# Two-level products of a fused attention and Fourier-mix kernel: later sums made among the products, conversion not emptied at a chunk's end, three loaded blocks in the last unit

## The chip, the cores and the metric

The kernel runs on one core of a Trainium2 chip. A core has TensorE (matmuls; its weight loads are listed apart as PEld), VectorE (DVE), ScalarE (ACT), GpSimd (POOL) and SyncE (SP, which here only issues DMAs). The metric is device time in microseconds. The kernel before took 2447.19 us (median of three runs, 2444.5 to 2452.97).

## The reference, cut to what matters

An attention block (batch 8, 12 heads, 448 rows, head size 64, heads mixed before and after the softmax) makes `x`; a Fourier mix, a normalisation and a two-layer network follow. The change lies in the last lines alone.

```python
X = np.fft.fft(np.fft.fft(x, axis=1), axis=2)
u = x + np.real(X).astype(np.float32)
un = (u - mu) / np.sqrt(var + 1e-06)
ch = np.maximum(un @ w_ch1, 0.0) @ w_ch2      # 768 x 3072 and 3072 x 768, given as float64
return (u + ch).astype(np.float32)
```

## The kernel before, in words

**Tiles and stages.** First comes the attention with the Fourier mix (`mix_phase`). Then `ffn_phase` works through the network in six chunks of its 3072 inner columns (`NC = 6`); in each chunk it passes over the 3584 rows in seven blocks of 512 (`NTB = 7`). A chunk and a block make a unit `n`, with `c, t = divmod(n, NTB)`, 42 in all. A unit has two halves. `first` multiplies the block by the chunk's part of `w_ch1`, applies the ReLU and leaves the result in `h`; `second` or `second2` multiplies `h` by the chunk's part of `w_ch2` and adds the result to the output in DRAM.

**Products by sevens.** Both multiplications split each matrix in 2 x 2 and make seven products of sums of blocks in place of eight. The sums of the weights are made while they are converted from float64 (`_Weights`); those of the inner result are `hs1`, `hs2`, `h21` and `h12s` (lines 1066 to 1068 and 1078). From chunk 2 on (`DEEP = 2`), the second multiplication is split once more: each of the seven products is made as seven again of half the size (`second2`). For this the four sums of each of the seven inner blocks are needed, `hq` (`quarter`, line 990), and of the weights `wt` (`halves`, line 999, in the first unit of a chunk, in turn on VectorE and GpSimd).

**The order.** From chunk 2 on the program writes out the order of TensorE, VectorE, ScalarE and GpSimd by hand; each engine takes its instructions in that order. `second2` gives each piece of work a step `s`. Product `j` of `ORDER2` begins at step `7 j` and makes its seven matmuls at `7 j` + 0, 3, 4, 5, 8, 13 and 16, so that three products overlap; at the same steps ScalarE copies sums out of PSUM (`take`, line 1185), VectorE adds to them (`more`, line 1179), and whole results are added (`both`, line 1188). The matmul at `7 j + 16` adds to the PSUM sum `P` that `more(j, 3, "P")` of step `7 j + 11` reads, and so must wait for it. Steps from 49 on are made during the next unit's first half, at the places that `SEAM` gives (the seam). An output block goes out as a DMA that adds to DRAM, from GpSimd's queue (`out_`, line 1191).

**Sums of the inner result, before.** After product 6 of the first half GpSimd makes the four sums of H11 and H22 together (128 x 256 each). After product 2 VectorE makes `hs1`, `hs2` and `h21` and at once the four sums of H21, HS1 and HS2 together (128 x 384 each). After the last product VectorE makes `h12s`, and GpSimd the four sums of H12 and H12S. All of VectorE's share stands in front of the adds of `second2`.

**Conversion.** A part of a weight matrix (25 parts for chunks 1 to 5) is converted on VectorE in 32 instructions (lines 235 to 267): four pieces of seven, and four sums. `wts.add` queues a part, `wts.deal(n)` issues the next `n` instructions, and with them loads, and stores left from the call before. Those DMAs go through GpSimd's queue up to chunk 1, later through SP's. Chunk 1 deals 18 in the first half and 28 in the second and queues ten parts in its seven units; two-level units but the first of a chunk deal 18 (`DEALS`, after products 0 to 4). After the first half of a two-level chunk's last unit, `wts.deal(1000)` issues whatever is queued. In that unit too the next chunk's weights are loaded, in the buffers that its products leave (`load_w1`, `load_w2`).

**The last unit.** (`end`.) Two output blocks are loaded and added to in SBUF: (0, 0) in the tile of product 1 and (0, 1) in that of product 2, the last of all. They are stored at the end without adding DMAs; (1, 0) and (1, 1) go out as adding DMAs. GpSimd makes two of the whole-tile adds, at steps 34 and 47, both into the tile of the last product.

## Time and profile before

| what | value |
|---|---|
| median of three runs | 2447.19 us (2444.5 to 2452.97) |
| the profiled execution's own time | 2442.24 us |
| its span, from first to last instruction | 2440.46 us |
| mean granted TensorE clock | 0.981 |
| busy: PE, PEld, DVE, ACT, POOL | 2324.3, 1749.7, 1707.8, 1130.4, 1099.9 us |
| TensorE's first matmul of the network | 861.2 us from the span's start |
| first unit of chunk 1, of chunk 2 | 1151.33 us, 1408.55 us |

Engines are named PE, PEld, DVE, ACT, POOL and SP; `L1179` is line 1179 of the kernel before. A line of the timeline gives start, duration, engine, line, operation, output and inputs, shapes and count, and in brackets the idle time ahead with what ended it. A stretch in the table by stage is given in microseconds from the span's start. Durations of successive instructions can overlap a little, so the distance from start to start is used where several are added up.

### The profile page before, as it was taken

How to read it: one execution, taken by the hardware profiler on the slowest of the kernel's cores; microseconds unless marked ns; L12 is line 12 of the kernel's file. 1: busy time of each engine (PE TensorE's matmuls, PEld its weight loads, DVE VectorE, ACT ScalarE, POOL GpSimd, SP SyncE). 2: the span in 40 equal slices, each digit the busy share in tenths (PEclk: the TensorE clock that was granted, in tenths of full speed). 3: DMA queues.
4: the chain of work that ended last, by engine and by line, in shares of the span. 5: the costliest groups of instructions: out<-in, count | busy, mean ns of one | idle time of the engine just before them, and what ended most of it. 6: DMA issues, size and time to landing. Idle time of an engine off the chain costs nothing.

```text
span 2440.5 us, 59595 instructions
## 1 busy us (share of the span) xinstructions
PE 2324.3 (95%) x22856; PEld 1749.7 (72%) x22856; DVE 1707.8 (70%) x3414; ACT 1130.4 (46%) x3097; POOL 1099.9 (45%) x1557
## 2 busy tenths in 40 slices
PE   6999999999999699999999999998999899999998
PEld 3555555555555477677777689987899789998997
DVE  4888888888897557775676667676767677555445
ACT  4776777666677332231222234433344244344443
POOL 3697787977777241210334242233323333333323
PEclk8999999999999899999999999998999899999999
DMA  7555564655554645658687865575655946674553
GB/s 168 167 177 171 179 189 158 186 171 171 175 165 155 214 152 193 212 177 308 184 231 193 273 186 136 163 212 172 182 135 144 261 111 167 159 201 103 143 117 65
DMA packets 216616, 428.65 MB, mean 176 GB/s; under 512 B 39054, under 2 KB 138406, under 8 KB 216334
## 3 DMA queue, kind: packets, MB, share of 16 engines
q1 hardware_dynamic: 146574, 286.38, 34.1%
q0 software_dynamic: 63904, 136.70, 25.6%
q8 instruction: 183, 3.00, 0.5%
q10 hardware_dynamic: 5856, 1.77, 0.4%
q14 instruction: 99, 0.81, 0.1%
HBM read 212.76 MB, written 129.39 MB: 140 GB/s over the span
## 4 chain that ended last, share of the span: by engine, by line
PE 78%; DVE 11%; DMA 5%; ACT 2%; POOL 2%; issue 1%; SPq 1%; ACTq 0%; DVEq 0%; POOLq 0%
PE psP L1026 14%; PE psP L1159 8%; PE psR L1026 7%; PE mx L486 6%; PE psP L1102 6%; PE ms L547 5%; PE ms L459 5%; PE po L520 5%; PE psR L1159 4%; PE psQ L1026 4%; DMA Kr<-Sb 3%; PE psR L1102 3%; DVE hq L990 2%; PE psQ L1159 2%; PE ms L661 2%; PE psQ L1102 1%
## 5 line engine op out<-in xcount | busy, mean ns | idle before, releaser
L1026 PE MATMUL psP<-ub,w1t 128*128 128x256 f32 x2016 | 481.6, 380 | 0.0
L1026 PEld LDWEIGHTS psP<-ub,w1t 128*128 128x128 f32 x2016 | 380.3, 191 | 48.6 <-issue 0.6
L510 POOL TENSOR_SCALAR PP<-PP,rcp 128x448 f32<-128x448 f32 x384 | 254.5, 672 | 219.5 <-DVE rcp L508 188.1
L500 ACT ACTIVATE PP<-mx,nmx 128x448 f32<-128x448 f32 x384 | 240.7, 632 | 162.9 <-DVE nmx L493 151.3
L1191 POOL DMA_DIRECT2D out_dram<-od x110 | 134.5, 1416 | 361.9 <-DVE od L1179 163.5
L493 DVE TENSOR_REDUCE nmx<-mx 128x1 f32<-128x448 f32 x384 | 223.0, 617 | 86.7 <-PE mx L486 84.9
L486 PE MATMUL mx<-Kr,kw 60*32 60x448 f32 x3072 | 231.8, 550 | 16.7 <-DMA Kr<-Sb 12.8
L1026 PE MATMUL psR<-ub,w1t 128*128 128x256 f32 x1008 | 231.3, 379 | 0.0
L1188 DVE TENSOR_TENSOR od<-od 128x768 f32<-128x768 f32 x194 | 186.6, 973 | 55.2 <-ACT od L1185 54.2
L990 POOL TENSOR_TENSOR hq<-h 128x256 f32<-128x256 f32 x112 | 83.6, 746 | 305.2 <-issue 169.2
L531 DVE STREAM_TRANSPOSE Pv<-po 128x896 f32<-128x896 f32 x192 | 212.7, 1108 | 9.4 <-PE po L520 6.5
L520 PE MATMUL po<-PP,kw 60*32 60x448 f32 x3072 | 213.3, 539 | 2.9 <-POOL PP L510 2.0
L1185 ACT COPY od<-psP 128x192 f32<-128x192 f32 x388 | 124.3, 320 | 186.1 <-PE psP L1159 185.2
L1026 PEld LDWEIGHTS psR<-ub,w1t 128*128 128x128 f32 x1008 | 191.4, 190 | 25.9
L459 PE MATMUL ms<-kT,qT 64*32 64x448 f32 (+1 forms) x3072 | 202.6, 544 | 7.2 <-ACT qT L330 6.3
L330 ACT COPY Sb<-ms 124x448 f32<-124x448 f32 x384 | 184.0, 542 | 36.1 <-DMA Kr<-Sb 21.4
L547 PEld LDWEIGHTS ms<-Pv,vv 64*64 64x64 f32 x5376 | 143.5, 133 | 69.9 <-issue 33.8
L213 POOL DMA_DIRECT2D raw<-in_moe_w_ch_dram x80 | 48.8, 612 | 262.9 <-DVE tmp L257 252.0
L547 PE MATMUL ms<-Pv,vv 64*64 64x120 f32 x5376 | 166.3, 269 | 0.3 <-issue 0.2
L1102 PE MATMUL psP<-w2t,h 128*128 128x384 f32 x448 | 155.2, 490 | 2.2 <-DVE od L1122 2.2
L1159 PE MATMUL psP<-wt,h 128*128 128x192 f32 x392 | 101.5, 341 | 43.4 <-DVE od L1179 43.4
L1045 DVE TENSOR_TENSOR h<-h,psP 128x512 f32<-128x512 f32 x42 | 28.9, 688 | 161.6 <-PE psP L1026 161.3
(140 smaller groups left out, 4516.9 us busy)
## 6 DMA issues: line engine op xcount, KB each, us to landing
ub<-ub SPq DMA_DIRECT2D x294, 384.0 KB
Kr<-Sb SPq DMA_DIRECT2D x768, 105.0 KB
out_dram<-od POOLq DMA_DIRECT2D x138, 384.0 KB, 6.6
w1t<-w SPq DMA_DIRECT2D x42, 384.0 KB
w2t<-w SPq DMA_DIRECT2D x42, 384.0 KB
raw<-in_moe_w_ch_dram POOLq DMA_DIRECT2D x48, 256.0 KB, 5.3
raw<-in_moe_w_ch_dram POOLq DMA_DIRECT2D x32, 384.0 KB, 7.3
w<-wst POOLq DMA_DIRECT2D x84, 128.0 KB, 3.6
```

Source lines behind the costliest of these rows:

```text
L459: nc.tensor.matmul(pss[x][o:o + hi - lo, :S], st["qT", xx][64 * x:64 * x + 64, y, lo:hi], st["kT", xx][64 * x:64 * x + 64, y, :], start=Tr ...
L486: nc.tensor.matmul(mx[x][64 * z + o:64 * z + o + 32, :S], kw1[64 * x:64 * x + KR, o:o + 32], Kr[64 * x:64 * x + KR, z, :], start=True, sto ...
L493: nc.vector.tensor_reduce(nmx[:, :], steps[T]["mx"][x][:, :S], axis=AX.X, op=ALU.max, negate=True)
L500: nc.scalar.activation(steps[T]["PP"][:, x, :], steps[T]["mx"][x][:, :S], ACTF.Exp, bias=steps[T]["nmx", x][:, :], accum_out=steps[T]["den ...
L510: nc.gpsimd.tensor_scalar(PP[:, x, :], PP[:, x, :], rcp[:, x:x + 1], 1.0, op0=ALU.mult, op1=ALU.mult)
L520: nc.tensor.matmul(po[o:o + 32, z, :S], kw2[64 * z:64 * z + KR, y, :], PP[64 * z:64 * z + KR, :, c * HS:(c + 1) * HS], start=True, stop=True)
L531: nc.vector.transpose(g["Pv"][:, T % GT, :].rearrange("p (z s) -> p z s", z=2), steps[T]["po"][:, :, :S])
L547: nc.tensor.matmul(pss[y][64 * x:64 * x + 64, :nu * R], st["v", pr][64 * y:64 * y + 64, x, jb * D:(jb + 1) * D], _ap(Pv, 64 * y * rp + 32 ...
L1026: nc.tensor.matmul(p[:, m, :], w1[i][:, kc, m * P:(m + 1) * P], ub[:, kc, :], start=i in (0, 4, 1)[:3 - seed] and m == kc == 0, stop=kc == ...
L1102: nc.tensor.matmul(p, h[:, LHS[i], kf, x * P:(x + 1) * P], w2[i][:, kf, :], start=i in (0, 4, 1)[:3 - (c > 0)] and kf == 0, stop=kf == FM ...
L1159: nc.tensor.matmul(ps[j, key][:, :DQ], a, b, start=m in (0, 4), stop=True, skip_group_check=True)
L1188: eng.tensor_tensor(D[j][:, :, :], D[j][:, :, :], D[k][:, :, :], op=ALU.add)
```

## The change

- **Conversion.** `wts.deal(1000)` at the end of the two-level chunks is gone, and that at the end of chunk 1. Chunk 1 deals 24 in the first half (4 for 3) beside 28 in the second, and queues parts until there are 52 instructions: twelve parts in place of ten. Two-level units deal 14 in place of 18, and the first of a chunk 8 in place of none. A last `deal(0)` issues stores that are left.
- **Sums.** `quarters` makes the four sums of one or more blocks at once. In front of the second half VectorE makes only those of HS2 (128 x 128 each), between `hs2` and `h21`. Those of H21 come at step 12 of `second2` and those of HS1 at step 19, both on VectorE; `h12s` at step 20. GpSimd makes those of H12 right after the last product of the first half, without waiting for `h12s`, and those of H12S after step 20.
- **Last unit.** Three blocks are loaded in tiles of their own: (0, 0), (0, 1) and (1, 1). The last product adds into the tile of (0, 1); product 1 is copied out by ScalarE and added as a whole. VectorE makes seven whole-tile adds in place of five, GpSimd two (steps 34 and 41, into two tiles), and (1, 1) is stored, at step 48, where it went out as an adding DMA. The pool of output tiles has nine buffers in place of seven.

```diff
-DEALS = (2, 4, 4, 4, 4, 0, 0)
+DEALS = ((0, 2, 2, 2, 2, 0, 0), (2, 3, 3, 3, 3, 0, 0))
...
-    def quarter(eng, hq, h, f0, f1, s):
+    def quarters(eng, hq, h, f0, f1):
...
-                    for x in range(4):
-                        quarter(nc.gpsimd, hq, h, H11, H22 + 1, x)
+                    quarters(nc.gpsimd, hq, h, H11, H22 + 1)
...
-            if deep and t:
-                wts.deal(DEALS[k])
-            elif i != 2 and not deep:
-                wts.deal(2 if norms else 3)
+            if deep:
+                wts.deal(DEALS[t > 0][k])
+            elif i != 2:
+                wts.deal(2 if norms else 3 if c == 0 else 4)
             if i == 2:
                 vec.tensor_tensor(hs1, h21, h22, op=ALU.add)
                 vec.tensor_tensor(hs2, hs1, h11, op=ALU.subtract)
+                if deep:
+                    quarters(vec, hq, h, HS2, HS2 + 1)
                 vec.tensor_tensor(h21, h11, h21, op=ALU.subtract)
-                if deep:
-                    for x in range(4):
-                        quarter(vec, hq, h, H21, HS2 + 1, x)
...
-        vec.tensor_tensor(h12s, h12, hs2, op=ALU.subtract)
         if deep:
-            for x in range(4):
-                quarter(nc.gpsimd, hq, h, H12, H12S + 1, x)
-        if t == NTB - 1 and deep:
-            wts.deal(1000)
+            quarters(nc.gpsimd, hq, h, H12, H12 + 1)
+            wts.deal(0)
+        else:
+            vec.tensor_tensor(h12s, h12, hs2, op=ALU.subtract)
...
         def part(j, q):
+            if end and j == 6:
+                j = 8
...
-            if end and j in (5, 6):
+            if end and j == 6:
                 more(j, q, key)
...
+        v11, v12, v22 = range(7, 10)
+        on(12, lambda: quarters(vec, st["hq"], st["h"], H21, H21 + 1))
+        on(19, lambda: quarters(vec, st["hq"], st["h"], HS1, HS1 + 1))
+        on(20, lambda: vec.tensor_tensor(st["h"][:, H12S], st["h"][:, H12],
+                                         st["h"][:, HS2], op=ALU.subtract))
+        on(20, lambda: quarters(pl, st["hq"], st["h"], H12S, H12S + 1))
         if end:
-            on(0, load, j1, 0, 0)
-            on(0, load, j2, 0, 1)
-            for s, *o in ((19, vec, j1, j0), (33, vec, j5, j0), (34, pl, j2, j5),
-                          (40, vec, j6, j5), (41, vec, j3, j6), (47, vec, j6, j4),
-                          (47, pl, j2, j4)):
+            for v, r, d in ((v11, 0, 0), (v12, 0, 1), (v22, 1, 1)):
+                on(0, load, v, r, d)
+            for s, *o in ((24, vec, v11, j0), (33, vec, j5, j0), (34, pl, v12, j5),
+                          (40, vec, j6, j5), (41, vec, j3, j6), (41, pl, v22, j6),
+                          (47, vec, v22, j4), (48, vec, v12, j4), (54, vec, v11, j1)):
                 on(s, both, *o)
             on(42, out_, j3, 1, 0)
-            on(48, out_, j6, 1, 1)
-            on(7 * j1 + 19, store, j1, 0, 0)
-            on(7 * j2 + 19, store, j2, 0, 1)
+            on(48, store, v22, 1, 1)
+            on(55, store, v11, 0, 0)
+            on(61, store, v12, 0, 1)
...
-            for _ in range(0 if c == 0 else 2 if t < 3 else 1):
+            while c and sum(o[1] for o in wts.ops) < 52:
                 wts.add(*parts_.pop(0))
...
-            if c == 0 or t == NTB - 1:
+            if c == 0:
                 wts.deal(1000)
...
-                for name, bufs in (("wt", 1), ("hq", 1), ("od", 7)):
+                for name, bufs in (("wt", 1), ("hq", 1), ("od", 9)):
...
-            while parts_ and sum(o[1] for o in wts.ops) < sum(DEALS):
+            while parts_ and sum(o[1] for o in wts.ops) < 14:
                 wts.add(*parts_.pop(0))
```

More of the change, by code (lines that the diff above doesn't have):

```diff
@@ L985, in quarter @@
                               for x in range(2) for f in range(2))
-        to, a, b, op = ((o[:, :, 0], a21, a22, ALU.add),
-                        (o[:, :, 1], o[:, :, 0], a11, ALU.subtract),
-                        (o[:, :, 2], a11, a21, ALU.subtract),
-                        (o[:, :, 3], a12, o[:, :, 1], ALU.subtract))[s]
-        eng.tensor_tensor(to, a, b, op=op)
+        for to, a, b, op in ((o[:, :, 0], a21, a22, ALU.add),
+                             (o[:, :, 1], o[:, :, 0], a11, ALU.subtract),
+                             (o[:, :, 2], a11, a21, ALU.subtract),
+                             (o[:, :, 3], a12, o[:, :, 1], ALU.subtract)):
+            eng.tensor_tensor(to, a, b, op=op)
     def halves(i, eng):
```

## The prediction

> **What bounds the kernel now.** I read the page first, then who waited for whom on TensorE from the first two-level unit to the end, then a table by stage whose stretches are units. A unit is 512 rows of one chunk; its length is from its first matmul of line 1026 to the next unit's.
>
> ```profile
> span 2440.5 us, 59595 instructions
> ```
>
> ```profile
> PE psP L1159 <- DVE od L1179: 44.2, 30, 12.5
> ```
>
> The change touches only what follows the attention: one-level chunk 1 and two-level chunks 2 to 5. In the latter TensorE loses 44.2 us in 30 waits, all for line 1179: the VectorE add that reads a PSUM sum before matmul 3 of the same product may add to it. So VectorE's lateness at one place is the loss, not its load.
>
> The stages; columns are stretch and length, busy time of PE, PEld, DVE, ACT, POOL, granted clock, DMA share, GB/s:
>
> ```profile
> 1151.33:1368.47 217.14, 217.14 (x841) 159.60 (x840) 141.87 (x335) 53.36 (x101) 78.77 (x114) 1.00 0.77 209
> 1368.47:1408.55 40.08, 37.89 (x142) 27.08 (x141) 27.60 (x66) 8.96 (x17) 9.39 (x13) 0.97 0.90 302
> 1408.55:1444.59 36.04, 33.50 (x175) 30.79 (x174) 17.88 (x34) 14.64 (x41) 19.23 (x27) 0.99 0.58 167
> 1444.59:1618.58 173.99, 172.36 (x912) 159.16 (x911) 121.17 (x246) 74.97 (x211) 53.13 (x60) 1.00 0.59 157
> 1618.58:1669.89 51.31, 37.26 (x184) 34.41 (x183) 35.47 (x70) 14.97 (x43) 11.16 (x12) 0.87 0.80 250
> 1669.89:1708.51 38.62, 36.05 (x184) 33.41 (x183) 25.19 (x48) 15.00 (x43) 21.11 (x24) 0.96 0.56 137
> 1708.51:1883.12 174.61, 172.36 (x912) 159.15 (x911) 124.29 (x246) 74.98 (x211) 53.52 (x60) 1.00 0.59 156
> 1883.12:1932.52 49.40, 37.45 (x184) 34.60 (x183) 32.21 (x70) 14.98 (x43) 10.77 (x12) 0.86 0.82 254
> 1932.52:1971.24 38.72, 36.15 (x185) 33.51 (x184) 25.20 (x48) 15.00 (x43) 21.09 (x24) 0.96 0.56 135
> 1971.24:2180.46 209.22, 206.83 (x1093) 190.97 (x1093) 135.50 (x251) 89.87 (x253) 64.12 (x72) 1.00 0.61 166
> 2180.46:2219.19 38.73, 36.16 (x185) 33.51 (x184) 25.18 (x48) 15.00 (x43) 21.09 (x24) 0.96 0.55 136
> 2219.19:2392.61 173.42, 172.36 (x911) 159.15 (x911) 87.86 (x156) 74.95 (x211) 52.62 (x60) 1.00 0.48 117
> 2392.61:2440.46 47.85, 36.48 (x192) 32.92 (x190) 22.43 (x45) 13.28 (x37) 17.24 (x16) 0.92 0.44 83
> ```
>
> Five quiet units of chunk 5 take 173.42 us with PE busy 172.36: 34.47 us is a unit without a gap (172.36 / 5). Against that, chunk 2's last unit is 16.84 too long and chunk 3's 14.93; the first units of chunks 3, 4 and 5 are 4.15, 4.25 and 4.26 too long, and chunk 2's has 2.54 idle; the other 21 units before the last, in four rows, are 1.63 + 2.25 + 2.40 + 1.06 = 7.3 too long. The gaps behind this, on TensorE's timeline (a drain, another, a chunk's first unit, an ordinary unit; the fifth row is matmul 3 of the third product of that ordinary unit):
>
> ```profile
> 1656.45 1.01 PE L1159 MATMUL psP<-wt,h 128*128 128x192 f32 x2 [12.54 <-DVE od L1179]
> ```
> ```profile
> 1918.89 1.01 PE L1159 MATMUL psP<-wt,h 128*128 128x192 f32 x2 [10.53 <-DVE od L1179]
> ```
> ```profile
> 2206.68 0.59 PE L1159 MATMUL psP<-wt,h 128*128 128x192 f32 x2 [2.57 <-DVE od L1179]
> ```
> ```profile
> 2416.47 0.59 PE L1159 MATMUL psP<-wt,h 128*128 128x192 f32 x2 [0.21 <-DVE od L1179]
> ...
> 2421.12 0.49 PE L1159 MATMUL psP<-wt,h 128*128 128x192 f32 x2
> ```
>
> A gap of 2.57 makes a unit 4.26 longer, for the clock falls after it. Two pairs of neighbouring stretches:
>
> ```profile
> 1429.68:1433.10 3.42, 1.54 (x10) 1.25 (x8) 3.35 (x9) 1.22 (x4) 0.61 (x1) 1.00 0.02 7
> 1433.10:1436.51 3.41, 2.75 (x17) 2.75 (x18) 1.66 (x6) 1.58 (x5) 2.83 (x4) 1.00 0.00 0
> 2204.51:2207.92 3.41, 1.24 (x7) 1.24 (x8) 2.61 (x9) 0.61 (x2) 1.40 (x2) 1.00 0.01 2
> 2207.93:2211.33 3.40, 3.40 (x12) 3.40 (x12) 0.71 (x2) 1.27 (x5) 1.41 (x3) 0.50 0.01 2
> ```
>
> 1.88 us idle in such a stretch (3.42 - 1.54) left the clock at 1.00; 2.17 (3.41 - 1.24) was followed by one at 0.50. [...]
>
> **The parts of the change, one by one.** *The drain.* Lines 1082 and 1083, which empty the conversion at a chunk's end, go. At the end of chunks 2 and 3 they put 20 conversion instructions (18 dealt in each of six units out of four steps of 32) between the first half's sums and the add of line 1179: the gaps of 12.54 and 10.53, smaller ones ahead, and the half clock behind. All of 16.84 + 14.93 = 31.8 us goes if the work finds cover. It moves to three places. (a) Chunk 1 deals 52 a unit for 46: 6 more at 0.42 (141.87 / 335) are 2.5 us, beside 12.5 us in which VectorE idles per unit ((217.14 - 141.87) / 6). TensorE has no gap there, so this costs nothing; without that cover it would be 2.5 x 7 = 18. GpSimd issues these loads and stores, in order behind the accumulating writes, as now. (b) Ordinary two-level units deal 14 for 18, which only helps. (c) First units of chunks deal 8, now none:
>
> ```profile
> 2195.01 0.69 DVE L1045 TENSOR_TENSOR h<-h,psP 128x512 f32<-128x512 f32 x1 [3.28 <-PE psP L1026]
> 2197.50 0.69 DVE L1051 TENSOR_TENSOR h<-h,psR 128x512 f32<-128x512 f32 x1 [1.80 <-PE psR L1026]
> ...
> 2201.92 0.83 DVE L990 TENSOR_TENSOR hq<-h 128x384 f32<-128x384 f32 x1
> ...
> 2204.48 0.35 DVE L999 TENSOR_TENSOR wt<-w2t 128x192 f32<-128x192 f32 x1
> ...
> 2205.67 0.69 DVE L1078 TENSOR_TENSOR h<-h 128x512 f32<-128x512 f32 x1
> 2206.28 0.35 DVE L1179 TENSOR_TENSOR od<-od,psP 128x192 f32<-128x192 f32 x1
> ```
>
> Six fall into the 3.28 us idle before line 1045 and two into the 1.80 after it: at 0.42, 2.5 and 0.8. At the 0.6 of the drain (12.54 / 20) 3.6 would overrun the first by 0.3, which the second takes up. Their loads and stores stand on SP behind the weight loads of the seam and before the next `ub` loads; SP would wait only if VectorE fell behind, and the DMA share is 0.56 there against 0.80 in the unit they leave. The last dealt step, in chunk 4's last unit, stores chunk 5's weights during the fifth product of seven, a whole half before they are loaded.
>
> *The sums in ordinary units.* The front is what VectorE does between the last ReLU it waits for and the first add of line 1179:
>
> ```profile
> 2413.45 0.56 DVE L990 TENSOR_TENSOR hq<-h 128x384 f32<-128x384 f32 x1
> ...
> 2415.46 0.69 DVE L1078 TENSOR_TENSOR h<-h 128x512 f32<-128x512 f32 x1
> 2416.06 0.35 DVE L1179 TENSOR_TENSOR od<-od,psP 128x192 f32<-128x192 f32 x1
> ```
> ```profile
> L999 DVE TENSOR_TENSOR wt<-w2t,wt x32: 350/357/746, 1398.8 to 2205.4; 128x192 f32<-128x192 f32 x32
> ```
> ```profile
> L990 POOL TENSOR_TENSOR hq<-h x112: 712/726/1441, 1423.5 to 2417.7; 128x256 f32<-128x256 f32 x112
> ```
>
> Four sums of 384 take 2.01 us (2413.45 to 2415.46), `h12s` 0.60. In their place stand four of 128. No row has that size: 192 takes 0.35 and 384 0.56, so a straight line gives 0.28; bounds 0.2 and, with GpSimd in the way, 0.75 (the 746 of the row). I take 0.30, near the smallest row. The front shortens by 2.61 - 1.20 = 1.4 against a gap of 0.21 (up to 0.7 elsewhere), so it closes with 1.2 to spare. GpSimd's four sums of H12 now come earlier, beside these, and at 0.4 each (three overlaps) would eat that 1.2 and no more. Next in line is the sum of the second and third product: eight sums, `h12s` and three adds of 0.35 now stand between the first add and the third product's, 2.4 + 0.7 + 1.1 = 4.2 us, where TensorE needs 4.65 (2416.47 to 2421.12): they fit. GpSimd's four more, smaller instructions add at most 4 x 0.73 us per unit, of which it is busy for 10.5 (52.62 / 5) in 34.5. Of the 7.3 us I take 7.0; bounds 3 and 7.3.
>
> [...]
>
> *The sums in first units of a chunk.* There the front also holds four weight differences, and GpSimd works throughout, so four sums took 2.56 us (2201.92 to 2204.48). Four of 128 at the same 1.5-fold price (0.83 / 0.56) take 1.8; `h12s` (0.61) goes too: 1.4 less. GpSimd's H12 sums, now before and not after it, can lengthen the weight differences by 0 to 4 x 0.4; I take 0.2, for the row's median lies at its minimum. The gap falls from 2.57 to 1.4, below the 1.88 that left the clock whole. The four units together are 15.2 too long (4.15 + 4.25 + 4.26 + 2.54); 4 x 1.4 = 5.6 stay, 9.6 go. Bounds 0 and 12.4 (0.7 left in each).
>
> *Chunk 1's last unit.* 40.08 for 36.19 (217.14 / 6): VectorE stood for the new chunk's weights.
>
> ```profile
> 1398.30 0.36 DVE L999 TENSOR_TENSOR wt<-w2t 128x192 f32<-128x192 f32 x1 [4.80 <-DMA w2t<-w]
> ```
>
> Nothing in the change frees that load, and as many dealt instructions stand behind it (28 in the half for 26, though narrower). I take 0; bounds 3.9 gained and 4 lost, a second gap of that size with its clock.
>
> *The last unit.* Now the last product adds into a tile that GpSimd is adding to:
>
> ```profile
> 2428.55 2.26 POOL L1188 TENSOR_TENSOR od<-od 128x768 f32<-128x768 f32 x1
> ```
> ```profile
> 2430.84 0.35 DVE L1179 TENSOR_TENSOR od<-od,psQ 128x192 f32<-128x192 f32 x1 [1.78 <-POOL od L1188]
> ```
> ```profile
> 2432.04 0.59 PE L1159 MATMUL psP<-wt,h 128*128 128x192 f32 x2 [2.55 <-DVE od L1179]
> ```
> ```profile
> L1188 DVE TENSOR_TENSOR od<-od 128x768 f32<-128x768 f32 x194 | 186.6, 973 | 55.2 <-ACT od L1185 54.2
> ```
>
> After the change its last GpSimd add is one product earlier and into another tile. VectorE gets two whole-tile adds more (2 x 0.97) and gives four adds of 0.35 to ScalarE: 0.5 more. 2.55 - 0.5 is about 2.0; with its front's 0.2, 2.2. Bounds 0 and 3. The third loaded block is read during the first half and hidden there; two more buffers cost no time.
>
> *Sum.* 31.8 + 7.0 + 9.6 + 0 + 2.2 = 50.6 us. The profiled execution took 2442.24 (span 2440.46 and 1.8 around it), so 2391.6 like for like. The runs shown were 2444.5 to 2452.97, median 2447.19, 4.95 above the profiled one; with the same distance 2396.6, so I say 2396.
>
> **The rivals.** *Chunk starts stay.* GpSimd's earlier sums shut VectorE out, whole instructions at a time, where both are busiest: four times 0.4, plus a dealt store late. The gap stays above 2 us with its half clock, the 9.6 do not come, and chunk 1's end loses 2 more: 39 saved, 2408. For it: the 0.83 and 746 rows. Against: the median of 357. 20%.
>
> *More than I count.* Narrower conversions (256 wide, for 384) behind the weight wait close chunk 1's last gap (3.9), and chunk starts keep 0.7 only (2.8): 57.3 saved, 2390. 13%.
>
> *Slower: the sums among the products hold TensorE in all 28 units.* At s per 128-wide sum the third product's add comes 12 s - 5.3 us late: 8 s + 0.69 + 1.05 against 4.65, and at the front 4 s against 2.61 less its gap of 0.21. From s = 0.54 this costs over 1.2 per unit and so more than the 34 us that the drains and the last unit give; at 0.60 it is 1.9, the clock halves (4.26 - 2.57 = 1.7 more), and 28 x 3.6 - 34 is 67 more, 2514. For it: fixed costs could make 128 as dear as 384 (0.56). Against: 192 takes 0.35. 3%.
>
> *The work only moves.* The 20 instructions come up again in front of an add of line 1179, and the kernel stays at 2447. It would have to be in first units, whose idle 3.28 and 1.80 speak against it. 2%.
>
> **How the numbers follow.** My case has 62%, with 2389 to 2404 of its own: 4 us for chunk starts, 4 for chunk 1's end, 3 for ordinary units, not all one way. 20%, 13%, 3% and 2% for the others. The range takes in 2390 and 2408 and, as the runs spread by -2.7 and +5.8 about their median, ends at 2386 and 2412. About 0.3% (7 us) is what a measurement can tell from no change; faster holds the first three cases: 0.95, same 0.02, slower 0.03.
>
> **What would show it.** Right: the last units of chunks 2 and 3 at 34.5 to 35 with clock 1.00; ordinary units at 34.5; chunk starts at 35.5 to 36.5 without a half clock; chunk 1's last unit near 40; the last gap under 1 us; 128-wide sums on VectorE at 0.3. Wrong: waits for line 1179 at the second or third product, half-clock stretches at chunk starts, a wait for conversion stores in first units, or chunk 1's units over 36.2.

## The result and the profile after

| | before | after |
|---|---|---|
| median, us | 2446.59 (4 runs, 2444.5 to 2452.97) | 2385.86 (4 runs, 2384.69 to 2390.02) |
| the profiled execution, us | 2442.24 | 2384.91 |
| its mean granted clock | 0.981 | 0.991 |

The ratio is 0.9751, with a 95% interval of 0.9729 to 0.9772. The forecast was 2396 (2386 to 2412): the direction and the main mechanism held, and the time came out 0.14 us under the range.

Line 1178 of the kernel after is line 1179 of before (VectorE's add), 1156 is 1159 (the seven matmuls), 1187 is 1188, 1119 is 1122. The page of the kernel after:

```profile
span 2383.1 us, 59994 instructions
```

Who waited for whom on TensorE from chunk 1 to the end (us in total, times, longest):

```profile
PE psP L1156 <- DVE od L1178: 11.1, 6, 2.7
PE psP L1026 <- DVE h L1045: 0.2, 1, 0.2
```

Of 44.2 us in 30 waits, 11.1 in 6 are left. The stages, cut at the same places as before (stretch and length, busy time of PE, PEld, DVE, ACT, POOL, clock, DMA share, GB/s):

```profile
1152.94:1370.57 217.63, 217.41 (x842) 159.52 (x840) 156.51 (x371) 53.38 (x101) 86.04 (x125) 1.00 0.82 221
1370.57:1406.78 36.21, 36.21 (x141) 26.52 (x140) 24.98 (x64) 8.96 (x17) 12.12 (x21) 1.00 0.95 319
1406.78:1441.75 34.97, 33.18 (x176) 30.53 (x175) 25.27 (x60) 14.64 (x41) 19.92 (x29) 1.00 0.66 196
1441.75:1612.77 171.02, 171.02 (x912) 159.28 (x911) 121.70 (x266) 74.98 (x211) 59.67 (x80) 1.00 0.60 158
1612.77:1646.97 34.20, 34.20 (x183) 31.85 (x183) 25.68 (x54) 14.99 (x43) 11.99 (x16) 1.00 0.93 285
1646.97:1684.12 37.15, 34.48 (x185) 31.84 (x183) 32.21 (x64) 15.01 (x43) 22.20 (x28) 1.00 0.65 173
1684.12:1855.14 171.02, 171.02 (x912) 159.29 (x911) 121.22 (x266) 74.98 (x211) 59.89 (x80) 1.00 0.59 155
1855.14:1889.34 34.20, 34.20 (x183) 31.85 (x183) 23.71 (x54) 14.99 (x43) 12.03 (x16) 1.00 0.92 286
1889.34:1925.88 36.54, 34.48 (x185) 31.84 (x183) 30.89 (x64) 15.00 (x43) 22.26 (x28) 1.00 0.65 165
1925.88:2131.11 205.23, 205.23 (x1094) 191.15 (x1094) 150.16 (x319) 89.98 (x253) 73.72 (x96) 1.00 0.64 176
2131.11:2167.39 36.28, 34.47 (x183) 31.82 (x183) 26.32 (x56) 14.99 (x43) 21.22 (x28) 1.00 0.62 158
2167.39:2338.41 171.02, 171.02 (x912) 159.28 (x911) 93.81 (x196) 74.97 (x211) 59.24 (x80) 1.00 0.51 123
2338.41:2383.13 44.72, 36.18 (x192) 32.97 (x190) 25.02 (x51) 14.55 (x41) 17.99 (x19) 0.95 0.41 80
```

Where length and PE's busy time agree, TensorE never waited. They agree in all ordinary two-level units and in both last units that used to drain, at 34.20 us a unit. Length less busy time is the gap: 1.79, 2.67, 2.06 and 1.81 us at the starts of chunks 2 to 5. The two tables, row against row:

| part | before to after, us | saved | forecast |
|---|---|---|---|
| last units of chunks 2 and 3 | 100.71 to 68.40 | 32.3 | 31.8 |
| 21 ordinary units | 731.24 to 718.29 | 12.9 | 7.0 |
| first units of chunks 2 to 5 | 152.11 to 144.94 | 7.2 | 9.6 |
| chunk 1's last unit | 40.08 to 36.21 | 3.9 | 0 |
| the last unit, to the span's end | 47.85 to 44.72 | 3.1 | 2.2 |
| chunk 1's six other units | 217.14 to 217.63 | -0.5 | 0 |
| all ahead of chunk 1 | 1151.33 to 1152.94 | -1.6 | 0 |
| sum | 2440.46 to 2383.13 | 57.3 | 50.6 |

The last line but one is not the change's doing. The part ahead of chunk 1 is the same in all kernels of this study, and its end lies anywhere from 1150.0 to 1160.0 us in their profiles. A spread of that size is in every comparison of whole runs, so the sections below also use the time from chunk 1's first matmul to the end: 1289.1 us before, 1230.2 after.

VectorE's sums of line 990 (ns: least, median, most):

```profile
L990 DVE TENSOR_TENSOR hq<-h x168: 275/284/676, 1425.9 to 2363.1; 128x128 f32<-128x128 f32 x168
```

A 128-wide sum takes 0.28 (forecast 0.30), but up to 0.676. Where, VectorE's timeline at the start of chunk 3 shows:

```profile
1667.83 0.56 DVE L990 TENSOR_TENSOR hq<-h 128x128 f32<-128x128 f32 x1
1668.43 0.63 DVE L990 TENSOR_TENSOR hq<-hq,h 128x128 f32<-128x128 f32 x1
1668.99 0.68 DVE L990 TENSOR_TENSOR hq<-h 128x128 f32<-128x128 f32 x1
1669.58 0.68 DVE L990 TENSOR_TENSOR hq<-h,hq 128x128 f32<-128x128 f32 x1
...
1671.05 0.60 DVE L999 TENSOR_TENSOR wt<-w2t 128x192 f32<-128x192 f32 x1
...
1672.63 0.35 DVE L999 TENSOR_TENSOR wt<-w2t,wt 128x192 f32<-128x192 f32 x1
1672.90 0.34 DVE L1178 TENSOR_TENSOR od<-od,psP 128x192 f32<-128x192 f32 x1
1673.16 0.28 DVE L990 TENSOR_TENSOR hq<-h 128x128 f32<-128x128 f32 x1
```

Four sums take 2.35 us (1667.83 to 1670.18, where the next instruction begins) for a forecast of 1.8, four weight differences 1.85 for 1.4 at 0.35 each. The first sum after them is at 0.28 again. At chunks 4 and 5 the four sums take 2.15 and 2.14 us, the four differences 1.85 and 1.86.

### The profile page after: what moved, and what is told of

The parts are those of the page before. It is cut to its first block, busy times and chain, and to the rows that moved or that the text cites. A ratio compares the mean times of both kernels' runs of the same rounds, so it can differ in the third digit from the quotient of the medians.

```text
span 2383.1 us, 59994 instructions
## 1 busy us (share of the span) xinstructions
PE 2307.2 (97%) x22856; PEld 1740.8 (73%) x22856; DVE 1739.4 (73%) x3636; ACT 1131.5 (47%) x3101; POOL 1145.6 (48%) x1684
## 4 chain that ended last, share of the span: by engine, by line
PE 85%; DMA 4%; DVE 4%; POOL 2%; issue 2%; ACT 1%; SPq 1%; ACTq 0%; POOLq 0%; DVEq 0%
PE psP L1026 17%; PE psP L1156 10%; PE psR L1026 9%; PE mx L486 7%; PE ms L547 6%; PE psP L1099 6%; PE ms L459 5%; PE po L520 5%; PE psR L1156 5%; PE psQ L1026 4%; PE psR L1099 3%; DMA Kr<-Sb 3%; PE psQ L1156 2%; PE ms L661 2%; PE psQ L1099 1%
## 5 line engine op out<-in xcount | busy, mean ns | idle before, releaser
L990 POOL TENSOR_TENSOR hq<-h 128x256 f32<-128x256 f32 (+1 forms) x168 | 104.3, 621 | 293.4 <-ACT h L1046 173.2
L1187 DVE TENSOR_TENSOR od<-od 128x768 f32<-128x768 f32 x196 | 188.6, 974 | 52.4 <-ACT od L1184 50.6
L459 PEld LDWEIGHTS ms<-kT,qT 64*32 64x32 f32 (+1 forms) x3072 | 67.9, 106 | 79.9 <-issue 51.8
```

The lines of the kernel that those rows point to most:

```text
L459: nc.tensor.matmul(pss[x][o:o + hi - lo, :S], st["qT", xx][64 * x:64 * x + 64, y, lo:hi], st["kT", xx][64 * x:64 * x + 64, y, :], start=Tr ...
L1187: eng.tensor_tensor(D[j][:, :, :], D[j][:, :, :], D[k][:, :, :], op=ALU.add)
```

## The experiments

The theory was that the moved sums closed the ordinary units' gaps, that 0.27 us of the forecast 34.47 belongs to the wait itself, and that the chunk starts are long because VectorE and GpSimd shut each other out (the sums of 0.56 to 0.68 us for 0.28 above). Its rivals lay the shorter units to the thinner dealing or to the two more output buffers, and the chunk starts to VectorE's own work there. What moved chunk 1's end was open. (In the expectations, "the planner" is what sets the order of instructions where chunk 1's work and chunk 2's meet; by what rule it does so stays open.) First the three edits alone, then the price of a gap, then chunk starts and chunk 1's end.

**The sums alone.** The kernel before, with the sums of the inner result moved and nothing else:

```diff
+                    quarters(vec, hq, h, HS2, HS2 + 1)
...
-            for x in range(4):
-                quarter(nc.gpsimd, hq, h, H12, H12S + 1, x)
+            quarters(nc.gpsimd, hq, h, H12, H12 + 1)
...
+        on(12, lambda: quarters(vec, st["hq"], st["h"], H21, H21 + 1))
+        on(19, lambda: quarters(vec, st["hq"], st["h"], HS1, HS1 + 1))
...
```

> Only the sums are moved; conversion, chunk ends and last unit as before. Theory A (a wait of TensorE costs its listed gap and some 0.27 us more, in which its pipeline of matmuls empties and fills): ordinary two-level units 34.20, as after the whole change, though only 0.21 to 0.7 of gap is removed from units of 34.7 to 35.2; together about 13 us. Theory B (the 0.27 below my gapless 34.47 comes from the fewer dealt instructions, the nine output buffers or other traffic): ordinary units at 34.47. Both: the last units of chunks 2 and 3 keep gaps of 11 and 9, chunk 1's last unit stays at 40.1, chunk starts fall to 36 to 37.5. Span 2417 by A, 2423 by B.

Measured: 2417.76 (before beside it 2443.66), ratio 0.9894, 0.9871 to 0.9918. Two of its stages: chunk 2's last unit, and the five ordinary units of chunk 5.

```profile
1620.85:1669.13 48.28, 36.69 (x184) 33.84 (x183) 35.79 (x78) 14.98 (x43) 11.76 (x16) 0.89 0.85 265
2200.44:2371.46 171.02, 171.02 (x912) 159.28 (x911) 93.90 (x196) 74.97 (x211) 59.30 (x80) 1.00 0.50 118
```

The drains stay, at 48.28 and 45.96, and the ordinary units are at 34.20: it is the sums that bring these down. The chunk starts take 34.96 and three times 36.29, without a half clock. Chunk 1's last unit takes 38.57, not the expected 40.1: its gap of 2.01 halved no clock.

**The conversion alone.**

```diff
-DEALS = (2, 4, 4, 4, 4, 0, 0)
+DEALS = ((0, 2, 2, 2, 2, 0, 0), (2, 3, 3, 3, 3, 0, 0))
...
-        if t == NTB - 1 and deep:
-            wts.deal(1000)
+        if deep:
+            wts.deal(0)
...
-            for _ in range(0 if c == 0 else 2 if t < 3 else 1):
+            while c and sum(o[1] for o in wts.ops) < 52:
...
```

> Only the conversion is changed; sums and last unit as before. Both theories: the last units of chunks 2 and 3 fall from 51.3 and 49.4 to 34.7. Theory A: ordinary units stay at 34.68, with the gap of 0.21; theory B: 34.4. On chunk 1's last unit: if its gap went because chunk 1 now converts other, narrower parts there, it falls from 40.1 to 36.2 in this kernel too; if the sums did it through the order that the planner chose at that seam, it stays at 40.1. Chunk starts at 38 to 39.5, with eight dealt instructions more and the old sums. Span about 2403.

Measured: 2411.39 beside 2443.66, ratio 0.9876, 0.9854 to 0.9899. Chunk 1's last unit, chunk 2's last, chunk 3's first, and the five ordinary ones:

```profile
1367.46:1403.84 36.38, 36.38 (x142) 26.52 (x141) 24.99 (x64) 8.96 (x17) 12.13 (x21) 1.00 0.94 316
1614.81:1649.62 34.81, 34.47 (x183) 31.83 (x183) 24.37 (x46) 14.99 (x43) 10.66 (x12) 1.00 0.93 289
1649.62:1690.38 40.76, 37.43 (x184) 34.79 (x183) 30.67 (x56) 15.00 (x43) 22.28 (x24) 0.92 0.58 150
2183.42:2356.86 173.44, 172.37 (x913) 159.16 (x912) 87.78 (x156) 74.97 (x211) 52.61 (x60) 1.00 0.49 117
```

The drains are gone, and chunk 1's end with them. The eight dealt instructions of a first unit aren't free: the gap at chunk 3's start rises from 2.57 (38.62 - 36.05) to 3.33. Of the four starts, 37.40, 40.76, 38.77 and 37.05, only the third lies in the expected 38 to 39.5. And the bare price of a wait stands in these rows: 34.47 busy in 34.81 us, 0.27 over the 34.20 of a unit without a gap, beside a gap of 0.34.

**The last unit alone.**

```diff
-            on(48, out_, j6, 1, 1)
+            on(48, store, v22, 1, 1)
...
-                for name, bufs in (("wt", 1), ("hq", 1), ("od", 7)):
+                for name, bufs in (("wt", 1), ("hq", 1), ("od", 9)):
```

(with the other lines of the last unit in the change.)

> Only the last unit and the nine output buffers. The last unit shortens by 2.6 (after the whole change it was 3.1 shorter, 0.5 of it the gap in its front), all else stays: ordinary units 34.68. Were the buffers behind the 0.27 (theory B), ordinary units would be at 34.4 and the span 6 us shorter still. Span 2437.8 by A, 2431 by B.

Measured: 2440.31 beside 2443.66, ratio 0.999, 0.9975 to 1.0004: not told from no change by the runs. By its profile the last unit went from 47.85 to 45.28, the 2.6 less that were expected; the five ordinary units:

```profile
2220.28:2393.71 173.43, 172.36 (x912) 159.15 (x911) 87.85 (x156) 74.96 (x211) 52.65 (x60) 1.00 0.50 121
```

They are as before, so the two buffers more aren't what shortened them.

From chunk 1's first matmul the three alone gain 29.2, 35.6 and 1.7 us, 66.5 together; 6.5 of the sums' 29.2 come out of the drains (51.31 to 48.28, 49.40 to 45.96), which the conversion edit takes anyway. The 60.0 left is near the 58.9 of the whole change.

**What a gap costs.** The kernel after, with one of VectorE's sums ahead of the first add repeated 6 to 26 times in the ordinary units of chunks 4 and 5 (a repeat writes the same result again):

```diff
+LADDER = {29: 6, 30: 10, 31: 14, 32: 18, 33: 22, 34: 26, 36: 8, 37: 12, 38: 16, 39: 20, 40: 24}
...
+                for _ in range(LADDER.get(n, 0)):
+                    vec.tensor_tensor(hq[:, HS2, 3], h[:, HS2, 1, :P], hq[:, HS2, 1],
+                                      op=ALU.subtract)
```

> The changed kernel, in which VectorE repeats one sum of 128 (the last of HS2, with the same result) a number of times in the front of the 11 ordinary units of chunks 4 and 5: 6, 10, 14, 18, 22, 26 and 8, 12, 16, 20, 24 times. The first 6 or 7 should cost nothing (the spare time that I worked out is 1.2 to 1.5 us), each further one 0.2. Theory A: a unit takes 34.20 + gap + 0.27 for any gap, so a step of 0.27 at the first gap and slope 1. Theory B: 34.20 + gap. Half clock: where over about 2 us idle fall into one stretch of 3.41 us, 1.6 more; where the gap straddles two stretches, none, as in the chunk start whose gap of 2.67 left the clock whole.

Measured: one run, 2456.98. A repeat cost 0.33, not the 0.2 assumed, so that six of them already made a gap, and no unit between zero and six repeats was seen. Units with 6 repeats, 10, none (a chunk's start), and 8:

```profile
1922.69:1958.51 35.82, 34.48 (x185) 31.84 (x184) 25.53 (x60) 15.00 (x43) 12.05 (x16) 1.00 0.55 147
1958.51:1997.51 39.00, 36.15 (x184) 33.51 (x184) 28.21 (x64) 15.00 (x43) 12.00 (x16) 0.96 0.57 154
2168.76:2205.07 36.31, 34.48 (x185) 31.84 (x183) 26.34 (x56) 15.00 (x43) 21.23 (x28) 1.00 0.60 146
2205.07:2243.13 38.06, 36.15 (x184) 33.51 (x184) 21.34 (x48) 15.00 (x43) 11.88 (x16) 0.96 0.47 114
```

The gaps are 1.34, 2.85, 1.83 and 1.91 us. A gap of 1.34 or 1.83 costs itself and 0.27 or 0.28; one of 1.91 itself and 1.95. So a gap has two extra prices: 0.27 in each of these units, and, where about 1.9 us of idle time fall into one stretch of 3.41, the half clock. The stretches around the 1.83 and the 1.91:

```profile
2191.05:2194.45 3.40, 1.57 (x10) 1.27 (x9) 3.33 (x9) 1.03 (x4) 2.31 (x4) 1.00 0.25 86
2194.46:2197.87 3.41, 3.41 (x22) 3.41 (x22) 3.21 (x12) 2.29 (x8) 0.53 (x2) 1.00 0.00 0
2228.56:2231.97 3.41, 1.50 (x9) 1.35 (x9) 3.21 (x14) 0.93 (x4) 0.00 (x0) 1.00 0.00 0
2231.98:2235.38 3.40, 3.40 (x13) 3.40 (x12) 2.16 (x8) 1.18 (x4) 1.66 (x4) 0.50 0.00 0
```

1.83 us idle in a stretch of 3.40 left the clock whole (the next is at 1.00), 1.91 in one of 3.41 halved it for the next.

**Weight differences later.** The last of the seven parts of `halves` in a chunk's first unit goes behind the second product's add:

```diff
-            if deep and t == 0:
+            if deep and t == 0 and k < 6:
...
+        if t == 0:
+            on(26, halves, ORDER2[6], vec)
```

> The changed kernel; in the first unit of a chunk the four weight differences of the last product, which VectorE makes in the front, are made at step 26 of the second half. Theory A (the gaps of 1.8 to 2.7 that are left at chunk starts are the lateness of VectorE's front): the front is 1.85 to 2.2 us shorter and the gaps fall to 0 to 0.8; units of 34.2 to 35.3 for 36.3 to 37.2. Theory B (something else is late next: the differences now stand before the adds of the fourth and fifth product, or the GpSimd sums are): a wait of 1 us or more appears at a later product, and the units stay over 36.

Measured: one run, 2381.84; 1223.0 us from chunk 1's first matmul. The starts of chunks 2 to 5 are 33.11, 34.53, 34.67 and 34.43 (34.97, 37.15, 36.54 and 36.28 after). With the four weight differences out of the front the gaps are as good as gone; chunk 1's last unit got a gap of 0.89 instead.

**GpSimd's H12 sums later.** In first units alone, behind step 20, where `h12s`'s sums stand:

```diff
-            quarters(nc.gpsimd, hq, h, H12, H12 + 1)
+            if t:
+                quarters(nc.gpsimd, hq, h, H12, H12 + 1)
...
+        if t == 0:
+            on(20, lambda: quarters(pl, st["hq"], st["h"], H12, H12S + 1))
...
```

> The changed kernel; in the first unit of a chunk GpSimd makes the sums of H12 only with those of H12S, behind h12s, as before the change. Theory A (GpSimd's sums shut VectorE out for whole instructions): the four weight differences in the front take 1.2 us for 1.85, the gaps at chunk starts fall by 0.6 to 0.7, while the four sums of HS2 stay at 0.56 to 0.68 each, for GpSimd's own weight differences run beside them. Theory B (the differences are slow for another reason): no change. The later sums of H12 (3.6 us for eight) could make product H12 wait, which would show as a wait of TensorE for GpSimd.

Measured: one run, 2383.22. The gaps fall to 0.88, 1.66, 1.14 and 0.89, by 0.9 to 1.0 each. VectorE's timeline at the place of the one shown of after:

```profile
1671.46 0.74 DVE L999 TENSOR_TENSOR wt<-w2t 128x192 f32<-128x192 f32 x1
1672.24 0.36 DVE L999 TENSOR_TENSOR wt<-w2t,wt 128x192 f32<-128x192 f32 x1
...
1672.78 0.35 DVE L999 TENSOR_TENSOR wt<-w2t,wt 128x192 f32<-128x192 f32 x1
1673.05 0.35 DVE L1179 TENSOR_TENSOR od<-od,psP 128x192 f32<-128x192 f32 x1
```

The weight differences but the first are back at 0.35, and the four take 1.59 us to the add (line 1179 here) for 1.85. At chunk 4 the two add up to the gap's fall of 0.92: the differences take 1.19 for 1.85, and the four sums 1.89 for 2.15. VectorE's instructions are the same in number and size; only GpSimd's sums went from beside them.

**Chunk 1's conversion as before.** Two-level units keep their gain, chunk 1 deals and queues as before:

```diff
-                wts.deal(2 if norms else 3 if c == 0 else 4)
+                wts.deal(2 if norms else 3)
...
-            while c and sum(o[1] for o in wts.ops) < 52:
+            for _ in range(0 if c == 0 else 2 if t < 3 else 1):
```

(with the rest dealt in later units, 17 for 14.)

> The changed kernel, but chunk 1 deals and queues as before (46 a unit, ten parts, so that its last unit converts 384 wide), and two-level units deal 17 for 14 to make up. Theory A (chunk 1's last gap went because narrower instructions and fewer weight differences now stand ahead of the adds there): it comes back, 39 to 40 us for 36.2. Theory B (the sums or the planner's order elsewhere closed it): it stays at 36.2. Ordinary units 34.2 to 34.5, since 17 dealt leave VectorE less spare time.

Measured: one run, 2398.2; 1237.0 us from chunk 1's first matmul. Chunk 1's last unit is 37.17 with a gap of 0.72, between the two theories' 39 to 40 and 36.2: four weight differences, not eight, stand ahead of the add here too (table below). A few ordinary units with 17 dealt instructions rise to 34.9 to 36.3.

**Weight differences earlier and later.** Four of the seven parts one product earlier or more, the last one as in the experiment above:

```diff
-                halves(ORDER2[k], (nc.vector, nc.gpsimd)[k % 2])
+                for x in ((0,), (1,), (2,), (3,), (4, 5), (), ())[k]:
+                    halves(ORDER2[x], (nc.vector, nc.gpsimd)[x % 2])
...
+        if t == 0:
+            on(26, halves, ORDER2[6], vec)
```

> As late_w, and GpSimd's last four weight differences of a chunk's first unit stand one product earlier, ahead of its sums of H11 and H22 and not beside VectorE's front. Theory A: VectorE's sums of HS2 there fall from 0.56 to 0.68 each towards 0.28 to 0.45, the gaps vanish, and the four units take 34.2 to 34.6 each: about 9 us less than the changed kernel. Against it: GpSimd's sums of H11 come up to 2.4 us later, and TensorE could wait for them at step 3 of the first product.

Measured: one run, 2378.8; 1223.0 us from chunk 1's first matmul. The start of chunk 3:

```profile
1647.04:1681.68 34.64, 34.50 (x183) 31.80 (x183) 31.54 (x64) 15.02 (x43) 22.78 (x28) 1.00 0.70 186
```

0.14 us of gap is left there, and none at chunks 4 and 5 (34.39 and 34.46 us, all busy). The four sums of HS2 did not come down to the expected 0.28 to 0.45: at chunk 3 they take 0.70, 0.70, 0.54 and 0.28. And with the last part alone made later, the time from chunk 1's first matmul was the same 1223.0, so that the earlier GpSimd part shows no gain. Chunk 1's last unit is 37.35.

**The kernel after once more,** timed beside the two that follow:

> The changed kernel once more, for the comparison with the next one on the same chip: ratio to the kernel before 0.973 to 0.977, span 2382 to 2386.

Measured: 2385.52 (5 runs, 2382.64 to 2388.24) beside 2443.16, ratio 0.9765, 0.9749 to 0.978. The starts of chunks 3 and 4 took 38.46 and 38.20, for 37.15 and 36.54 in the first profile of the same kernel. The gap at chunk 4, here and in the first profile (second fence):

```profile
1913.60:1917.00 3.40, 1.35 (x8) 1.05 (x7) 3.33 (x9) 0.75 (x3) 2.24 (x4) 0.99 0.40 161
1917.01:1920.41 3.40, 3.40 (x12) 3.40 (x12) 2.82 (x11) 1.28 (x4) 0.59 (x2) 0.51 0.02 5
```
```profile
1910.56:1913.97 3.41, 2.43 (x15) 2.13 (x14) 3.34 (x8) 1.60 (x6) 3.33 (x6) 1.00 0.78 298
1913.98:1917.38 3.40, 2.33 (x14) 2.33 (x15) 3.33 (x14) 1.35 (x5) 0.27 (x1) 1.00 0.04 14
```

2.05 us idle in one stretch, and the clock is halved; 0.98 and 1.07 us, the same gap cut by the boundary, and it stays. That boundary, where no clock changes, is an estimate: in the profile of after the clock rises at 883.21 us and next falls at 2378.25, which is 438 steps of 3.4133 us, and 136 of them back from 2378.25 lies 1914.0 us, and 207 back 1671.7, in the gap at chunk 3.

**Both starts and the end.** The weight differences as above; two of the last unit's adds and a store later; in chunk 1's last unit the dealt instructions moved towards the end:

```diff
-            wts.deal(2 if norms and k >= NT2 else 4)
+            wts.deal(2 if norms and k >= NT2 else
+                     (2, 2, 2, 2, 6, 6, 8)[k] if n == DEEP * NTB - 1 else 4)
...
-                          (47, vec, v22, j4), (48, vec, v12, j4), (54, vec, v11, j1)):
+                          (53, vec, v22, j4), (54, vec, v12, j4), (54, vec, v11, j1)):
...
-            on(48, store, v22, 1, 1)
+            on(53, store, v22, 1, 1)
```

> late_early with two more edits: in the last unit VectorE makes the adds that TensorE waits for ahead of the whole-tile adds of steps 47 and 48, and chunk 1's last unit deals 2 instructions for 4 after each of the first four products of the second half and the rest after the last three. From the units measured: chunk starts 34.2 to 34.6 (late_early gained 8 us there), chunk 1's last unit 36.2 for the 37.35 of late_early, the last unit 0.7 shorter because VectorE no longer idles 0.65 for GpSimd. Span 2375, some 9 us (0.4%) less than the changed kernel. Should the adds at the end only change places, the last unit stays at 44.7 to 45.0; should the planner put other work ahead of the adds at chunk 1's end, the gap of 0.9 stays.

Measured: 2383.3 (5 runs, 2379.85 to 2390.28) beside 2443.16, ratio 0.9759, 0.9739 to 0.9779, and so not told from the kernel after. Chunk 2's first unit:

```profile
1409.83:1449.40 39.57, 36.07 (x175) 32.61 (x174) 27.35 (x67) 14.62 (x41) 19.45 (x31) 0.91 0.56 163
```

Chunk 1's last unit had no gap (36.19), but the dealt instructions came up in the next unit, whose first-half matmuls waited 3.5 us for VectorE. The last unit is 44.87, as in the kernel after (44.72), though the wait ahead of its last matmuls is gone:

```profile
2375.47 0.56 PE L1158 MATMUL psP<-wt,h 128*128 128x192 f32 x2
```

They start 35.83 us into the unit, for 38.36 in the kernel after, and the end does not move.

**No dealing in first units.**

```diff
-DEALS = ((0, 2, 2, 2, 2, 0, 0), (2, 3, 3, 3, 3, 0, 0))
+DEALS = ((0, 0, 0, 0, 0, 0, 0), (2, 4, 4, 3, 3, 0, 0))
```

> The changed kernel, but the first unit of a two-level chunk deals nothing, as before the change, and the others 16. Theory A (the gap at chunk 1's end hangs on how many weight differences of the next unit the planner puts ahead of the adds, and the eight dealt instructions keep the third product's four behind them): eight differences stand there again and the gap is back at about 2 us less the 0.6 of the narrower conversions, 38 us for 36.2. Theory B (the narrower conversions alone): it stays at 36.2. The starts of chunks 3 and 4 fall to the 36.3 of chunk 5, which deals nothing, for 37.15 and 36.53: the price of the eight dealt instructions.

Measured: one run, 2392.37. Chunks 3, 4 and 5 start with 36.28, 36.29 and 36.28 us: the eight dealt instructions cost 0.87 and 0.25 at chunks 3 and 4 and nothing at 5, where none were dealt. Chunk 1's last unit, though, is 41.56 with a gap of 3.42, for the expected 38. VectorE's timeline there, in this kernel, and (second fence) in the kernel after:

```profile
1402.08 0.36 DVE L999 TENSOR_TENSOR wt<-w2t 128x192 f32<-128x192 f32 x1 [4.16 <-DMA w2t<-w]
...
1408.01 0.36 DVE L999 TENSOR_TENSOR wt<-w2t 128x192 f32<-128x192 f32 x1 [2.42 <-DMA w2t<-w]
...
1409.22 0.55 DVE L1119 TENSOR_TENSOR od<-od,psP 128x384 f32<-128x384 f32 x1
```
```profile
1400.07 0.36 DVE L999 TENSOR_TENSOR wt<-w2t 128x192 f32<-128x192 f32 x1 [4.83 <-DMA w2t<-w]
...
1403.50 1.01 DVE L1119 TENSOR_TENSOR od<-od,psP 128x384 f32<-128x384 f32 x2
```

Between the first weight difference (line 999) that waits for its load and chunk 1's add (line 1119) stands, here, a second one with a load of its own to wait for, 2.42 us; in the kernel after it comes behind the add. So read, the kernels stand in one order (counts between the wait and the add, from VectorE's timelines):

| kernel | weight differences | dealt instructions | gap, us |
|---|---|---|---|
| before; the last unit alone; the sums alone | 8 | 8, 384 wide | 2.19; 2.52; 2.01 |
| no dealing in first units | 8 | 7 | 3.42 |
| chunk 1's conversion as before | 4 | 8, 384 wide | 0.72 |
| weight differences later; earlier and later | 4 | 7 (the load 1.1 us later) | 0.89; 0.89 |
| after; the conversion alone; H12 sums later | 4 | 7 | none |
| both starts and the end | 4 | 0 | none |

**Weight differences earlier and later, timed:**

> late_early again, now timed, since the two edits added in best gave nothing. From chunk 1's first matmul to the end it took 1222.9 us, the changed kernel 1230.2 and 1232.9; 7 to 10 us less than 2385.5 is 2376 to 2379, a ratio to the kernel before of 0.972 to 0.9735 where the changed kernel had 0.9751 and 0.9765. If the starts of chunks were not what is left to gain, it stays at 0.975 to 0.977.

Measured: 2382.04 (6 runs, 2371.77 to 2392.01) beside 2436.13, ratio 0.9767, 0.9739 to 0.9795. From chunk 1's first matmul its two profiles show 1223.0 and 1222.5, those of the kernel after 1230.2 and 1233.5: 7 to 11 us shorter where the change lies. The times of whole runs, which hold the spread ahead of chunk 1, do not show it: the ratio is that of the kernel after (0.9751 and 0.9765), not the expected 0.972 to 0.9735. So the gain rests on two profiles of each kernel.

## Why the prediction was wrong by a little

The sum came out 6.7 us larger than forecast: 5.9 from the ordinary units, 3.9 from chunk 1's end, 0.9 from the last unit and 0.5 from the drains, less 2.4 at the chunk starts and 2.1 lost up to the end of chunk 1's first six units.

**The drain: right.** Both last units run at 34.20 with clock 1.00, 32.3 for 31.8, and the conversion edit alone brings them to 34.81 and 34.74. The work found its cover in ordinary units and nearly so in chunk 1: six units took 217.63, or 36.27 each, just over the 36.2 that the prediction named as a sign of being wrong, but 217.14, as before, in other kernels that convert the same there (the conversion alone, H12 sums later). In first units the eight dealt instructions cost the 0.87 and 0.25 above, where the prediction placed them in idle time at no cost.

**The failed step: "34.47 us is a unit without a gap (172.36 / 5)".** It is a unit with one gap, less the gap's listed time. Busy time runs to the modelled ends of matmuls, and it still held 0.27 us for each wait, which goes when the wait goes: units without one are 34.20 (after, and with the sums alone), units with one have 34.47 or 34.48 busy, whatever its length, as long as the clock stays whole (0.34 with the conversion alone, 1.34 and 1.83 in the ladder, 2.67 at chunk 3). Over 21 units that is 5.7 us, nearly all of 12.9 - 7.0. The mechanism of that step held: 128-wide sums at 0.28, no wait at the second or third product, and the rival whose sums hold TensorE, from 0.54 a sum, is far off.

**Chunk starts: direction right, too much hoped.** The forecast gap of 1.4 measured 1.8 to 2.7, so 7.2 us went and not 9.6. The terms that failed are "the same 1.5-fold price" for the four sums, which was 2.14 to 2.35 for 1.8, the "0.2" for the weight differences, which lost 0.45 (1.85 for 1.4), and at chunks 3 and 4 the dealt instructions (0.87 and 0.25). The first rival's mechanism was there, at a part of its price: taking GpSimd's H12 sums away gave 0.9 to 1.0 back, and the gaps fell below the forecast 1.4 at all starts but chunk 3's (1.66); with the weight differences out of the front they were nearly gone. GpSimd's sums beside the four differences shown for the kernel after (1671.05 to 1672.63):

```profile
1670.65 0.78 POOL L990 TENSOR_TENSOR hq<-hq,h 128x128 f32<-128x128 f32 x1
1671.40 0.56 POOL L990 TENSOR_TENSOR hq<-h 128x128 f32<-128x128 f32 x1
1671.92 0.57 POOL L990 TENSOR_TENSOR hq<-h,hq 128x128 f32<-128x128 f32 x1
```

The two engines' instructions end in turn: GpSimd's at 1671.43, 1671.96 and 1672.49, VectorE's differences of 0.60, 0.49 and 0.60 each 0.21 or 0.22 us after one of them; the fourth, which begins when GpSimd's last has ended, takes 0.35. At chunk 4 the differences fell from 0.60, 0.49, 0.60 and 0.34 to 0.35 or 0.36 each, with only GpSimd's sums moved. So a sum of GpSimd's beside a difference cost 0.14 to 0.25 us, for the 0.4 that was estimated from one row (746 less 357 ns). That no half clock stood in the first profile, as forecast, was luck: its gaps of 2.06 and 2.67 fell, by the estimate of the boundaries, across two of them (0.98 and 1.07 us on the two sides, 1.07 and 1.59), and the second profile has the half clock at chunks 3 and 4.

**Chunk 1's end: forecast 0, came 3.9.** "Nothing in the change frees that load" was right (the wait is 4.83 for 4.80), "as many dealt instructions stand behind it" looked at the wrong instructions. What counted was that the add has four weight differences ahead of it in place of eight (the second four took 1.20 us before, 1402.63 to 1403.83 on VectorE); the narrower conversions, and one fewer, are the smaller part, 0.9 (4.33 us from the wait's end to the add with chunk 1's conversion as before, 3.43 after). That the order moved because the eight instructions now dealt in chunk 2's first unit hold the later weight differences back is argued: taking them away brings the second group and its wait ahead of the add again, but why the two parts of the program interleave so stays open.

**The last unit: near in size, 3.1 for 2.2, by luck.** The step "2.55 - 0.5 is about 2.0" failed: it took the gap ahead of the last matmuls to be what the end waits for, and this gap to go ("under 1 us"). It only fell to 2.37:

```profile
2376.77 0.59 PE L1156 MATMUL psP<-wt,h 128*128 128x192 f32 x2 [2.37 <-DVE od L1178]
```

VectorE's wait for GpSimd there shrank from 1.78 to 0.65, but two whole-tile adds of its own (0.96 each) came between. Of the 3.1 us, 1.1 lie ahead of these matmuls (39.43 to 38.36 from the unit's start) and 2.1 behind them (8.42 to 6.36 to the end). Before, the chain that ended last held the last matmuls (2432.04); after, it runs through the whole-tile adds of GpSimd (2371.07) and VectorE (2373.69, 2374.95, 2376.63) and holds none of them. With the gap closed by moving two of these adds behind it the unit still took 44.87. Why the part behind the last matmuls became shorter, by the adds or by the stores, is not shown.

**The offset.** The median before was 4.95 above its profiled execution, and the prediction carried that over; after, it was 0.95. With 2442.24 - 50.6 + 0.95 the forecast would have been 2392.6. Of the 10.1 us between forecast and median, 6.7 are the sum's (57.3 - 50.6) and 4.0 the offset's; -0.6 comes from rounding 2396.6. The rival "more than I count" has the same sum of 57.3 and its 3.9 at chunk 1's end, but its chunk starts did not come; the ordinary units and the last one made that up.

## What to carry to other kernels

Take the length of a unit without waits from a stretch where length and busy time agree, not from busy time where there are waits: a wait costs more than the idle time listed for it (here 0.27 us more), and a short gap that comes in every unit is worth closing. Price an instruction by rows from the place it goes to, with the other engine at work (a 128-wide sum took 0.28 us, and up to 0.68 beside GpSimd's work), and when work is moved near the border of two hand-written parts, list what then stands ahead of the add that the next matmul waits for, with the loads that it waits for. Before pricing a gap near the end, ask whether the end waits for it at all. Where runs spread by more than the effect, compare the profiles from the point where the kernels begin to differ.

## What the runs showed of the hardware

A wait of TensorE in this sequence of 128 x 192 matmuls cost its listed idle time and 0.27 us. Of that, 0.10 is the first pair after a gap, at 0.59 for 0.49 (the rows at 2416.47 and 2421.12 in the prediction). A matmul is listed with 0.326 us at a distance of 0.163 to the next, so that the last one ahead of a gap stays busy 0.16 us longer than one that is followed at once; the two make 0.26.

Idle time of 1.83 us in a stretch of 3.40 left the clock at 1.00, 1.91 halved it for the whole next stretch, and a gap of 2.06 us or 2.67 us that a boundary cut in two, where the estimate puts it (0.98 and 1.07 us, 1.07 and 1.59), left it whole. Near 1.9 us the idle time alone does not decide. Two stretches of chunk 2's first unit, in the kernel with the last unit alone and in the one with chunk 1's conversion as before:

```profile
1430.78:1434.18 3.40, 1.48 (x9) 1.48 (x10) 2.36 (x8) 0.84 (x3) 1.64 (x3) 1.00 0.00 0
1434.80:1438.20 3.40, 1.54 (x10) 1.25 (x9) 3.33 (x9) 0.99 (x4) 2.29 (x4) 1.00 0.45 180
```

1.92 us idle in the first was followed by a stretch at 1.00, 1.86 in the second by one at 0.50. In these runs a little over half of a stretch in idle time (1.91 of 3.41 us, as above) sufficed for the half clock. The same kernel therefore runs the same unit in 36.54 or 38.20 us, by where the gap falls.
